# One pair's x by DMA transpose instead of TensorE, and a q transpose moved behind it in SP's queue

## Chip, cores and metric

One core of one Trainium2 chip. The metric is the device time of one execution in microseconds (us), taken over several executions, of which medians and ranges are given. In the profile's lines PE is TensorE, PEld its weight loads, DVE VectorE, ACT ScalarE, POOL GpSimd and SP SyncE, which issues most DMAs; a q behind the name means the engine's sequencer or its DMA queue. PSUM is the memory that TensorE writes its results to.

## The reference

Sliding-window attention over 8 batches and 8 heads, its output taken as 4608 rows of 512, and a two-layer network with an ELU on top. Cut to what matters:

```python
# q, k, v: (8, 8, 576, 64); |i - j| <= 32 may attend
scores = 1.0 / np.sqrt(D) * np.matmul(q, k.transpose(0, 1, 3, 2))
attn = softmax(np.where(mask, scores, -1e9))           # (written out in the reference)
x = (attn @ v).transpose(0, 2, 1, 3).reshape(B * S, H * D)      # (4608, 512)
h = x @ w_in                                           # (4608, 2048)
g = np.where(h > 0.0, h, np.exp(np.minimum(h, 0.0)) - 1.0)
out = g @ w_out                                        # (4608, 512)
```

## The kernel before

The network's work is 144 loop steps, eight for each tile of 256 rows. In each step TensorE does a first-layer block of eight matmuls (`mm1`), and a second-layer block of four (`mm2`) for the step two back. ScalarE makes the exponential `e_sb`, VectorE `m_sb` and `g_sb` of it. Attention runs ahead of the network in the gaps. It goes by pairs, a pair being 128 rows; two pairs make the x of one tile. `begin` says at which step a pair's scores are made; three or four steps later it is normalized, and its x (128 x 512) must be transposed, either on TensorE with a ScalarE copy out of PSUM, or by a DMA on SP's queue:

```python
    FIRST_TWO, FIRST_DMA, BACK_AT = 6, 10, 18
    begin = {4: 9, 5: 12, 6: 18, 8: 26, 10: 31, 12: 37}
    # ... (cut)
    for i in range(4, NPAIR):
        # ... (cut: scores, exponential, mask, pv of the pair)
        n = kk + (3 + z if two else 2)
        at(n, "dve", normalize, i)
        if i < FIRST_DMA:
            at(n, "end", x_transpose, i)         # four TensorE transposes
            at(n, "end", x_evac, i, nc.scalar)   # ScalarE copies PSUM to SBUF
        else:
            at(n, "end", x_dma, i)               # one DMA transpose on SP
```

Pair 8 begins at step 26 and is normalized at step 29, pair 9 at step 30. Their tile is first read at step 32. The q and k of a later batch are cast, written to DRAM and brought back transposed by a DMA on SP:

```python
            if j0 == 12:
                at(free[n], "end", write_rows, b, which)
                at(free[n] + (3 if free[n] == 29 else 4), "mid",
                   transpose_rows, b, which)
```

For batch 3, q is written at step 24 and k at step 29, so their transposes are issued at steps 28 and 32.

The softmax here doesn't subtract the row's maximum and nothing guards it: scores larger than these inputs give would overflow.

## Time and profile before

| | before |
|---|---|
| device time, median of 3 executions | 305.11 us (304.83 to 305.93) |
| profiled execution (a fourth one, of 306.17 us), span in the trace | 304.5 us |
| TensorE busy | 296.0 us, 97% |
| TensorE's share of the chain that ended last | 90% |

The first table row is the metric. The span is the profiled execution as the trace sees it, from the first instruction to the last; it is some 1.7 us shorter than the device time of the same execution. The chain that ended last is followed back from the last instruction, at each step to what released it. As 90% of it is TensorE's work, what is taken from other engines only counts where TensorE waits for them. The lines behind this, and those of steps 28 to 32, are in the prediction.

### The profile page before, as it was taken

Reading aid. Unit: us, or ns where it says so; the run is one execution under the profiler, and the core shown is the slowest. Engines: PE = TensorE matmul, PEld = TensorE weight load, DVE = VectorE, ACT = ScalarE, POOL = GpSimd, SP = SyncE. Lnnn points to the kernel's source line nnn. Section 1 sums busy time; section 2 is a strip of 40 time slices with the busy share of each in tenths; the row PEclk is TensorE's granted clock in tenths of the full one; section 3 lists DMA queues with packets and bytes.
Section 4 is the critical chain, followed back from the end, with each engine's and each line's share of the span. In section 5 each row is a group of like instructions: output and inputs, shape, how many; then the busy total and the mean of one; then the engine's idle time right before and its main releaser. Section 6 shows DMA issues by size and latency. Waiting matters only on the chain.

```text
span 304.5 us, 7644 instructions
## 1 busy us (share of the span) xinstructions
PE 296.0 (97%) x3091; PEld 197.4 (65%) x3091; DVE 242.2 (80%) x473; ACT 168.6 (55%) x254; POOL 48.6 (16%) x68
## 2 busy tenths in 40 slices
PE   8789999999999999999999999999999999999995
PEld 3456666677676666666666666666667666666662
DVE  6867688978888887988798879887988787877664
ACT  3654556778664567546754675467535353534331
POOL 8836100910003100230013001400000000000000
PEclk9999999999999999999999999999999999999999
DMA  9999999998755997999799969996921111111011
GB/s 191 177 201 205 183 272 413 295 168 182 177 176 158 297 126 187 246 319 157 164 251 303 196 157 268 325 159 116 281 57 71 34 71 34 72 37 69 2 69 70
DMA packets 92117, 52.81 MB, mean 173 GB/s; under 512 B 76594, under 2 KB 81970, under 8 KB 92082
## 3 DMA queue, kind: packets, MB, share of 16 engines
q1 hardware_dynamic: 47330, 35.61, 43.3%
q0 software_dynamic: 42880, 10.10, 40.9%
q10 hardware_dynamic: 1872, 6.62, 5.8%
q8 instruction: 24, 0.39, 0.6%
q14 instruction: 11, 0.09, 0.1%
HBM read 36.70 MB, written 15.34 MB: 171 GB/s over the span
## 4 chain that ended last, share of the span: by engine, by line
PE 90%; DMA 3%; DVE 2%; POOL 2%; ACT 1%; issue 1%; DVEq 0%; POOLq 0%; ACTq 0%
PE ps L602 41%; PE psY L640 40%; PE psS L336 4%; PE psS L304 3%; DMA w_in_sb<-in_moe_w_in_dram 3%; PE ptx L279 1%; POOL Ve L142 1%; POOL c L136 1%; PE psXT L357 1%; DVE g_sb L626 1%; ACT pu L315 1%; DVE pm L324 0%; DVE m_sb L615 0%; PE ptx L274 0%; ACT e_sb L609 0%
## 5 line engine op out<-in xcount | busy, mean ns | idle before, releaser
L609 ACT ACTIVATE e_sb<-ps 128x512 f32<-128x512 f32 (+1 forms) x145 | 86.3, 595 | 120.6 <-PE ps L602 113.0
L602 PE MATMUL ps<-xT,w_in_sb 128*128 128x256 bf16 x1152 | 149.2, 273 | 1.4 <-DMA w_in_sb<-in_moe_w_in_dram 1.4
L640 PE MATMUL psY<-w_out_sb,g_sb 128*128 128x512 bf16 x576 | 147.6, 380 | 0.2 <-DVE g_sb L626 0.2
L602 PEld LDWEIGHTS <-w_in_sb 128*128 128x128 bf16 x1152 | 110.6, 98 | 39.7 <-DMA w_in_sb<-in_moe_w_in_dram 1.9
L626 DVE SCALAR_TENSOR_TENSOR g_sb<-ps,m_sb 128x512 bf16<-128x512 f32 (+1 forms) x145 | 99.4, 686 | 12.6
L615 DVE TENSOR_SCALAR m_sb<-e_sb 128x512 bf16<-128x512 f32 x144 | 62.5, 434 | 38.3 <-ACT e_sb L609 36.5
L640 PEld LDWEIGHTS <-g_sb 128*128 128x128 bf16 x576 | 54.5, 98 | 39.0 <-DVE g_sb L626 0.6
L142 POOL DMA_DIRECT2D Ve<-in_v_dram x40 | 35.4, 897 | 139.7 <-PE psS L336 79.9
L315 ACT ACTIVATE pu<-psS 128x1024 bf16<-128x1024 f32 x36 | 36.5, 1021 | 1.4 <-PE psS L304 1.4
L348 DVE TENSOR_TENSOR x_st<-psS,rc 128x512 bf16<-128x512 f32 x36 | 24.9, 692 | 1.2
L324 DVE TENSOR_TENSOR pm<-pu,masks 128x1024 bf16<-128x1024 bf16 x36 | 24.6, 683 | 0.6 <-ACT pu L315 0.5
L234 ACT CAST qkb<-f 128x768 bf16<-128x768 f32 (+1 forms) x29 | 25.0, 860 | 0.0
L336 PEld LDWEIGHTS <-pm 128*64 128x64 bf16 x576 | 11.2, 111 | 9.9 <-DVE pm L324 8.7
L336 PE MATMUL psS<-Ve,pm 128*64 128x65 bf16 x320 | 13.6, 197 | 0.9 <-DVE pm L324 0.9
L236 DVE COPY y_sb<-psY 128x512 f32<-128x512 f32 (+1 forms) x19 | 12.7, 671 | 1.0 <-PE psY L640 1.0
L304 PEld LDWEIGHTS <-kT 64*128 64x128 bf16 x576 | 9.5, 95 | 4.9 <-issue 4.0
L336 PE MATMUL psS<-Vo,pm 128*64 128x65 bf16 x256 | 12.0, 196 | 0.2 <-DVE Vo L153 0.2
L304 PE MATMUL psS<-qT,kT 64*128 64x64 bf16 x576 | 11.8, 191 | 0.5 <-DVE kT L236 0.5
L234 ACT COPY y_sb<-psY 128x512 f32<-128x512 f32 (+1 forms) x18 | 10.3, 571 | 3.0 <-DVE y_sb L236 3.0
L153 DVE COPY Vo<-Ve 64x1040 bf16<-64x1040 bf16 x24 | 10.3, 431 | 1.5 <-DMA Ve<-in_v_dram 0.8
L395 PE MATMUL ps_idle<-zeros 128*128 128x512 bf16 x27 | 9.5, 482 | 1.3 <-DVE zeros L194 1.3
L234 ACT COPY qT<-ptx 128x1152 bf16<-128x1152 bf16 (+2 forms) x8 | 7.5, 971 | 3.9 <-PE ptx L279 3.0
(36 smaller groups left out, 72.4 us busy)
## 6 DMA issues: line engine op xcount, KB each, us to landing
out_dram<-y_sb SPq DMA_DIRECT2D x35, 256.0 KB, 3.5
f<-in_q_dram SPq DMA_DIRECT2D x12, 576.0 KB, 5.6
f<-in_k_dram SPq DMA_DIRECT2D x12, 576.0 KB, 7.9
in_dram<-qkb ACTq DMA_DIRECT2D x10, 576.0 KB, 3.9
Ve<-in_v_dram POOLq DMA_DIRECT2D x24, 128.0 KB, 11.0
w_in_sb<-in_moe_w_in_dram POOLq DMA_DIRECT2D x4, 512.0 KB, 9.9
w_out_sb<-in_moe_w_out_dram POOLq DMA_DIRECT2D x4, 512.0 KB, 12.8
Ve<-in_v_dram POOLq DMA_DIRECT2D x16, 96.0 KB, 10.5
```

The source lines that it names most:

```text
L142: nc.gpsimd.dma_start(out=V_e[b % 3][p0:p1, m, :, 0:D], in_=v[b, :, lo + p0:lo + p1, :].rearrange("h p d -> p h d"))
L234: nc.scalar.copy(d_, s_)
L304: nc.tensor.matmul(psS[:, h % 2, hp * 128 + z * QB:hp * 128 + (z + 1) * QB], lhsT=kT[b % 2][base:base + 64, KPAD + hp * S + QB * qb - WIN: ...
L315: nc.scalar.activation(pu, _bap(psS, [psS.ap[0], [1, 1024]]), AX.Exp, scale=SCALE)
L324: nc.vector.tensor_mul(pm, pu, _bap(mm, [mm.ap[0], [0, H], [1, 2 * QB]]))
L336: nc.tensor.matmul(psS[QB * z:QB * (z + 1), par, hp * VD:(hp + 1) * VD], lhsT=pm[:, par * HP + hp, z * QB:(z + 1) * QB], rhs=vv[:, qb // 2 ...
L348: nc.vector.tensor_mul(x_st, _bap(psS, [psS.ap[0], [VD, HP], [512, 2], [1, D]]), _bap(rc, [rc.ap[0], [2, HP], [1, 2], [0, D]]))
L602: nc.tensor.matmul(ps[:, j, :], lhsT=w_in_sb[:, do, fo * 128:(fo + 1) * 128], rhs=xT[t][:, :, do, :], start=(do == 0), stop=(do == NDO - 1))
L609: nc.scalar.activation(e_sb, ps, AX.Exp)
L615: nc.vector.tensor_scalar(m_sb, e_sb, -1.0, None, ALU.add)
L626: nc.vector.scalar_tensor_tensor(g_t[kk][:, z * w:(z + 1) * w, :], ps, 0.0, m_t[kk][z], ALU.max, ALU.min)
L640: nc.tensor.matmul(psY[t][ts], lhsT=g_t[kk][:, j, ts * 128:(ts + 1) * 128], rhs=w_out_sb[:, s * FG + j, :], start=(s == 0 and j == 0), sto ...
```

## The change

The intent is to take four transposes off TensorE, which is the bound, and a copy off ScalarE. SP's queue is idle where the new DMA goes, and batch 3's q transpose, which holds it for 3.4 us just before, is put behind it.

```diff
         n = kk + (3 + z if two else 2)
         at(n, "dve", normalize, i)
-        if i < FIRST_DMA:
+        if i < FIRST_DMA and i != 8:
             at(n, "end", x_transpose, i)
             at(n, "end", x_evac, i, nc.scalar)
         else:
@@
-                at(free[n] + (3 if free[n] == 29 else 4), "mid",
+
+                at({24: 30, 29: 32}.get(free[n], free[n] + 4), "mid",
                    transpose_rows, b, which)
```

Only batch 3's q moves, from step 28 to 30. The empty line makes the line numbers after it greater by one: L602 of before is L603 of after, and so on.

## The prediction

> **What bounds the kernel now.** First the page: which engine is full, and what the chain that ended last is made of.
>
> ```profile
> PE 296.0 (97%) x3091; PEld 197.4 (65%) x3091; DVE 242.2 (80%) x473; ACT 168.6 (55%) x254; POOL 48.6 (16%) x68
> PE 90%; DMA 3%; DVE 2%; POOL 2%; ACT 1%; issue 1%; DVEq 0%; POOLq 0%; ACTq 0%
> ```
>
> TensorE is the bound: 90% of the chain is its own work, and outside the first 40 us it hardly ever stands still. So in the middle of the kernel the only things that count are the time its instructions take and the short waits between them. The change touches one place in the middle: loop steps 28 to 32. A step is one first-layer block (8 matmuls, L602), one second-layer block (4 matmuls, L640) and, in some steps, attention work. I found the steps from the program's order: the output copies of tile 2 end step 25, those of tile 3 step 33. So the block at 79.63 us is the first-layer block of step 29, those at 81.60, 83.70 and 86.17 are of steps 30, 31 and 32, and step 32 is the first that reads x of pairs 8 and 9 (tile 4).
>
> Second, the chain in order of time over these steps (start us, us, what). It gives TensorE's blocks with their pipelining taken out, so the pieces add up.
>
> ```profile
> 79.70 0.98 PE ps L602 x8
> 80.68 0.86 PE psY L640 x4
> 81.54 0.22 PE psXT L357 x4
> 81.77 0.87 PE ps L602 x8
> 82.64 0.86 PE psY L640 x4
> 83.50 0.36 PE psXT L357 x4
> 83.86 0.87 PE ps L602 x8
> 84.73 0.63 PE psS L304 x32
> ```
>
> The piece at 81.54 is the four transposes of pair 8, 0.22 us; the change takes it away. The piece at 83.50 is the same four transposes for pair 9, yet it lasts 0.36 us. The extra 0.14 us is a wait: TensorE arrives there before the data.
>
> Third, VectorE's timeline over the same time (start us, us, engine, line), to see when pair 9's x is made:
>
> ```profile
> 80.28 0.69 DVE L348 TENSOR_TENSOR x_st<-psS,rc 128x512 bf16<-128x512 f32 x1
> 81.34 0.43 DVE L615 TENSOR_SCALAR m_sb<-e_sb 128x512 bf16<-128x512 f32 x1 [0.37 <-ACT e_sb L609]
> 81.88 0.69 DVE L626 SCALAR_TENSOR_TENSOR g_sb<-ps,m_sb 128x512 bf16<-128x512 f32 x1
> 82.48 0.20 DVE L345 RECIPROCAL rc<-psS 128x8 f32<-128x8 f32 x1
> 82.72 0.69 DVE L348 TENSOR_TENSOR x_st<-psS,rc 128x512 bf16<-128x512 f32 x1
> ```
>
> Pair 8's x ends at 80.97. Pair 9's ends at 83.41, at the end of a chain that begins with step 29's first-layer block: its exponential on ScalarE (80.72 to 81.32), m_sb, g_sb, reciprocal, x_st. The weight load of pair 9's transposes then starts at 83.46, and the waits of this window (us in total, times, longest us) give how long the weight loader had stood:
>
> ```profile
> PEld L357 <- DVE x_st L348: 0.5, 1, 0.5
> ```
>
> Fourth, the SP queue's timeline:
>
> ```profile
> 76.68 3.44 SPq L265 DMA_TRANSPOSE qT<-in_dram  x1
> 86.36 1.96 SPq L265 DMA_TRANSPOSE kT<-in_dram  x1
> 90.08 0.93 SPq L665 DMA_DIRECT2D out_dram<-y_sb  x2
> 92.10 3.27 SPq L374 DMA_TRANSPOSE xT<-x_st  x2
> ```
>
> The queue is free from 80.12 to 86.36.
>
> **What the Trainium skill says.** "VectorE: DVE Perf Modes", The three transpose paths, puts a 128x128 bf16 transpose at 390 ns on TensorE, into PSUM, and at 1309 ns by DMA, into SBUF. The trace has TensorE shorter: 218 ns each, and four overlap to 0.22 us. For a DMA transpose of a pair it has 1.19 to 1.95 us of the issuing queue and 2.4 to 9.2 us to landing, median 2.8. So the DMA costs more time but no TensorE time. "DMA: Bandwidth & Descriptors", Issuing engines are not separate DMA queues, says that DMAs of all issuers share the same 16 engines and interleave. The trace agrees: x transposes issued in a quiet stretch land in 2.4 to 3.5 us, the one issued at 103.9 us, with 576 KB loads under way, in 6.4. [...]
>
> **The change, part by part.**
>
> *Removed on TensorE:* four transposes of pair 8, 0.22 us on the chain. *Removed on ScalarE:* the copy of pair 8 out of PSUM, 0.58 us at 81.80, with some 0.1 us of idle time in front of the cast behind it gone too.
>
> *What becomes of the 0.22 us.* Step 30's first-layer block starts at 81.54 in place of 81.77 and ends at 82.41; the second-layer block ends at 83.28. Then come pair 9's transposes, which need pair 9's x at 83.41. Does that x come earlier? Its chain starts from the end of step 29's first-layer block, which lies before the removed transposes, and nothing removed lies on it: step 29's exponential starts before the removed copy, and VectorE's five instructions stay. Worked out: block end 80.68, exponential done 81.32, m_sb 81.77, g_sb 82.57, reciprocal 82.68, x_st 83.41: 2.73 us, and 0.05 to the weight load. TensorE needs 0.86 + 0.87 + 0.86 = 2.59 us between the same two points without the removed transposes, 2.81 with them. So the wait that was 0.14 becomes 0.36, and the transposes of pair 9 stand where they stood: gain so far **0.00 us**.
>
> *What ScalarE's 0.6 to 0.7 us give.* The cast (0.84) moves from 82.28 to about 81.37, the write of k's rows to DRAM (0.57 on ScalarE's queue) from 83.15 to about 82.25, step 30's exponential from 83.83 to about 82.9. In the kernel before, that exponential (to 84.43) stands in front of pair 9's copy out of PSUM, which so ends at 84.90, while the scores of pair 11, into the same PSUM buffer, are due halfway through the piece at 84.73. That piece takes 0.63 us; the same 32 matmuls take 0.57 at 74.04, 96.63 and 106.86. After the change the copy can start at about 83.9 and end at 84.5, ahead of the scores: gain **0.06 us**.
>
> *Added on SP:* one DMA transpose, about 1.2 us of the queue, from 81.0. Nothing large is in flight then: the q transpose that was has moved, the batch-3 v loads were issued by 62 us and the next input loads come at 95.4. By the quiet cases it lands 2.4 to 3.5 us later, at 83.4 to 84.5. Step 32 needs it at 86.17, so 1.7 us are in hand: **0.00 us** on the path.
>
> *Moved on SP:* batch 3's q transpose, from 76.68 to about 82.2, behind x. Its issue (3.44) ends at 85.6, before k's transpose can start at 86.36 (which waits for the rows of k, written from about 82.25 rather than 83.15, and 3.9 us to landing in the median). With the median 5.9 us q lands at 88.1, k by about 91. The scores of pairs 12 and 13, the first to read them, come at 96.63. **0.00 us**.
>
> Sum: 305.11 - 0.06 = **305.05 us**. TensorE's work falls by 0.22 us, but 0.22 us of waiting takes its place.
>
> **Rivals.** *The whole 0.22 us counts, or 0.28 with the scores:* 304.8. For it: TensorE is the bound and the transposes are on the chain. Against it: the wait for pair 9's x 2 us later, already 0.14 us long. *The DMA is late:* x lands after 86.17. For it: landings up to 9.2 us are in this trace, and one of 6.4 from 81.0 gives 87.4, 1.2 us late: 306.3; 9.2 would give about 309. Against it: those fell among large loads; DMA moved 0 GB/s from 82 to 84 us. *The q transpose or the write of k's rows, now together, hold k up:* the write competes with q's 576 KB; SP's k would then start at 88 or 89 and push the output at 90.08 by a little. There are some 5 us in hand before the scores, so 305.1 still.
>
> **Range and chances.** The three runs spread over 1.1 us (304.83 to 305.93), which is more than the effect. I take 304.5 to 305.7: the low end is the first rival with the noise, the high end the noise and a little lateness. 2% is 6.1 us. Nothing in the change could give that much (the removed work is under 1 us on any engine), and only a landing later than any seen here could cost it: faster 0.005, same 0.985, slower 0.01.
>
> **What would show each step.** In the changed profile's chain the piece of pair 9's transposes grows from 0.36 to about 0.58 (wait plus work), with the weight load's wait for x_st from 0.5 to about 0.7; if it stays at 0.36 or shrinks, the step on the wait is wrong and the rival of 0.22 us holds. The scores piece shrinks from 0.63 to 0.57. ScalarE's exponential of step 30 starts some 0.9 us earlier against step 29's block. The new x transpose is at about 81.0 on SP and lands within 3.5 us; a wait of step 32's first-layer block for a DMA would show the late-DMA rival. The prediction fails as a time below 304.5 or above 305.7.

## The result and the profile after

| | before | after |
|---|---|---|
| device time, median of 5 executions each | 305.2 us (304.83 to 305.93) | 306.35 us (305.95 to 306.82) |
| ratio after to before | | 1.0036, 95% interval 1.0018 to 1.0053 |
| span of the profiled execution | 304.5 us | 304.6 us |

A ratio is the mean time of one kernel's fast runs over that of the other's of the same rounds, so it is not quite the ratio of the medians quoted. The two count as "same" (within 2%), as predicted, but the time lies above the predicted range: the change costs where a gain of 0.06 us was predicted. The results are correct. The spans differ by so little because the profiled execution of before happened to start slowly, as is shown below.

The page's busy line and chain shares of the kernel after:

```profile
PE 292.2 (96%) x3034; PEld 197.0 (65%) x3087; DVE 242.9 (80%) x473; ACT 168.4 (55%) x253; POOL 48.2 (16%) x68
PE 87%; DVE 4%; DMA 3%; POOL 2%; issue 2%; ACT 1%; DVEq 0%; POOLq 0%
```

The weight loads (PEld) tell what was removed: 3087 for 3091, four transposes. ScalarE has one instruction fewer. Of the 57 matmuls that PE seems to have lost, four are the removed transposes and the others missing records: a second trace of the kernel before has 3038.

**At the place of the change nearly all goes as the prediction has it.** The chain of the kernel after in order of time (start us, us, what):

```profile
79.14 0.99 PE ps L603 x8
...
80.16 0.61 ACT e_sb L610
...
80.79 0.44 DVE m_sb L616
...
81.32 0.69 DVE g_sb L627
82.01 0.12 DVE rc L345
...
82.16 0.70 DVE x_st L348
...
82.91 0.40 PE psXT L357 x4
83.31 0.87 PE ps L603 x8
84.18 0.57 PE psS L304 x32
```

The removed piece is gone. The chain now leaves TensorE at the end of step 29's first-layer block and runs through ScalarE and VectorE to pair 9's x (`x_st`), because TensorE now waits for this x. For that reason the piece of pair 9's transposes shows 0.40 us and not the 0.58 that the prediction gave as its sign: the chain counts the wait as VectorE's work. The weight loader's wait in the same stretch (us in total, times, longest us), 0.5 us before, is longer:

```profile
PEld L357 <- DVE x_st L348: 0.7, 1, 0.7
```

The scores piece shrank from 0.63 to 0.57 us, as predicted. SP's queue of the kernel after (start us, us, engine, line):

```profile
80.45 1.30 SPq L374 DMA_TRANSPOSE xT<-x_st  x1
81.86 4.15 SPq L265 DMA_TRANSPOSE qT<-in_dram  x1
86.05 2.26 SPq L265 DMA_TRANSPOSE kT<-in_dram  x1
```

The x transpose is issued at 80.45 us, and step 32's first-layer block, its first reader, starts at 85.72 right behind the work in front of it: nothing waits for the DMA. (The trace holds no landing time for this one; in p2, an experiment below, it is 3.57 us.)

**Where the time went.** To compare two traces over the whole kernel I use one marker per step: the start of that step's `g_sb` on VectorE. The difference between two kernels in the start of the same marker is constant where they run alike and jumps where one of them loses time. "c1" and "c2" are a second profile of the kernels before and after, on one chip.

| `g_sb` of step | after - before, us | c2 - c1, us |
|---|---|---|
| 29 | -0.56 | +0.58 |
| 33 | -0.61 | +0.52 |
| 61 | -0.62 | +0.53 |
| 66 | -0.50 | +0.65 |
| 95 | -0.39 | +0.76 |
| the last (step 143, second half) | -0.40 | +0.75 |
| end of the span | +0.16 | +1.29 |

The first row is the two kernels' different luck in the start-up, before the changed steps; it differs in sign between the two pairs of profiles. From there on both pairs say the same: a gain of 0.05 us at the place of the change, two losses of some 0.11 us around steps 62 and 91, and a loss of about half a us after the last marker. Together after loses 0.72 us in both pairs, none of it where the change is.

**The stall on VectorE.** VectorE's timeline at step 62 (start us, us, engine, line, operation; in brackets the idle time in front, and what the profile puts it down to). Before:

```profile
146.79 0.43 DVE L615 TENSOR_SCALAR m_sb<-e_sb 128x512 bf16<-128x512 f32 x1
147.33 0.69 DVE L626 SCALAR_TENSOR_TENSOR g_sb<-ps,m_sb 128x512 bf16<-128x512 f32 x1
```

After:

```profile
146.18 0.43 DVE L616 TENSOR_SCALAR m_sb<-e_sb 128x512 bf16<-128x512 f32 x1
147.06 0.69 DVE L627 SCALAR_TENSOR_TENSOR g_sb<-ps,m_sb 128x512 bf16<-128x512 f32 x1 [0.46 <-PE ps L603]
```

From m_sb's start to g_sb's start it is 0.54 us before and 0.88 after: g_sb is 0.34 us late. The releaser in brackets is an inference of the profile, and it can't be right: the `ps` that g_sb reads was read by the exponential that m_sb comes from. The same happens at step 91 (from 0.53 to 0.89 us). As g_sb is the last to read its PSUM buffer, a first-layer block two steps on has to wait, and 0.11 us of each stall reach TensorE.

**The end.** The last transfer of both kernels is an output DMA of ScalarE's queue. Before, then after:

```profile
301.77 0.36 ACTq L657 DMA_DIRECT2D out_dram<-y_sb  x1
```

```profile
301.37 0.36 ACTq L658 DMA_DIRECT2D out_dram<-y_sb  x1
```

After is 0.40 us ahead here, and ends 0.16 us later. The semaphore checks of SP on the kernel's last line show why (engine, operation, count: duration in ns, first and last start in us). Before, in the stretch 301.6 to 302.1 and then 303.0 to 303.8:

```profile
L712 SPq EVENT_SEMAPHORE  x6: 17/28/28, 301.7 to 302.0; - x6
...
L712 SPq EVENT_SEMAPHORE  x2: 28/28/28, 303.2 to 303.6; - x2
```

After, in the stretch 303.0 to 303.8; between 301.4 and 303.1 there is none:

```profile
L713 SPq EVENT_SEMAPHORE  x8: 28/28/28, 303.2 to 303.6; - x8
```

SP checks at the end that every DMA has completed, one semaphore after another in a fixed order. Before, it gets through most of them while the last output is in flight, and the last check passes as that output lands. After, it stands at the first check until the output lands, and has all others still to do. The traces name the semaphores: SP's checks go through 100, 102, 104, 105 and 115 to 118 in this order, and the last output is on 118 in the kernel before and on 100 in the kernel after. The waits of SP's queue over the end (us in total, times, longest us), before and after:

```profile
SPq L712 <- DMA out_dram<-y_sb: 1.4, 3, 0.7
```

```profile
SPq L713 <- DMA out_dram<-y_sb: 1.8, 1, 1.8
```

One wait in place of three is the sign that I looked for in the experiments. A second thing is late at the end: ScalarE's last DRAIN (a sequencer instruction), before and after, in the same form as SP's lines above:

```profile
L712 ACTq DRAIN  x1: 8/8/8, 303.9 to 303.9; - x1
```

```profile
L713 ACTq DRAIN  x1: 135/135/135, 304.3 to 304.3; - x1
```

### The profile page after: what moved, and what is told of

It is laid out like the page before. It is cut to its first block, busy times and chain, and to the rows that moved or that the text cites. A ratio compares the mean times of both kernels' runs of the same rounds, so it can differ in the third digit from the quotient of the medians.

```text
span 304.6 us, 7584 instructions
## 1 busy us (share of the span) xinstructions
PE 292.2 (96%) x3034; PEld 197.0 (65%) x3087; DVE 242.9 (80%) x473; ACT 168.4 (55%) x253; POOL 48.2 (16%) x68
## 3 DMA queue, kind: packets, MB, share of 16 engines
q1 hardware_dynamic: 47874, 35.74, 43.5%
## 4 chain that ended last, share of the span: by engine, by line
PE 87%; DVE 4%; DMA 3%; POOL 2%; issue 2%; ACT 1%; DVEq 0%; POOLq 0%
PE ps L603 40%; PE psY L641 38%; PE psS L336 4%; PE psS L304 3%; DMA w_in_sb<-in_moe_w_in_dram 3%; DVE g_sb L627 1%; PE ptx L279 1%; POOL Ve L142 1%; ACT e_sb L610 1%; DVE m_sb L616 1%; POOL c L136 1%; PE psXT L357 1%; DVE x_st L348 0%; DVE pm L324 0%; DVE Vo L153 0%
## 5 line engine op out<-in xcount | busy, mean ns | idle before, releaser
L603 PE MATMUL ps<-xT,w_in_sb 128*128 128x256 bf16 x1152 | 149.2, 273 | 0.3 <-DMA w_in_sb<-in_moe_w_in_dram 0.2
L641 PE MATMUL psY<-w_out_sb,g_sb 128*128 128x512 bf16 x526 | 139.3, 379 | 3.3 <-issue 0.8
L603 PEld LDWEIGHTS <-w_in_sb 128*128 128x128 bf16 x1152 | 110.8, 98 | 38.8 <-DMA w_in_sb<-in_moe_w_in_dram 0.7
L616 DVE TENSOR_SCALAR m_sb<-e_sb 128x512 bf16<-128x512 f32 x144 | 63.2, 439 | 36.2 <-ACT e_sb L610 34.3
L395 PE MATMUL ps_idle<-zeros 128*128 128x512 bf16 x24 | 8.6, 470 | 1.4 <-DVE zeros L194 1.3
```

Source lines behind the costliest of these rows:

```text
L603: nc.tensor.matmul(ps[:, j, :], lhsT=w_in_sb[:, do, fo * 128:(fo + 1) * 128], rhs=xT[t][:, :, do, :], start=(do == 0), stop=(do == NDO - 1))
L616: nc.vector.tensor_scalar(m_sb, e_sb, -1.0, None, ALU.add)
L641: nc.tensor.matmul(psY[t][ts], lhsT=g_t[kk][:, j, ts * 128:(ts + 1) * 128], rhs=w_out_sb[:, s * FG + j, :], start=(s == 0 and j == 0), sto ...
```

## The experiments

**My theory** after reading the traces: both losses come from how the program is numbered, not from the work. The compiled program's listing, which isn't printed here, shows that the DMAs of SP and ScalarE signal completion on eight semaphores in turn, in program order; the change adds one DMA at step 29, so every later DMA moves on by one, which the semaphores named above bear out. That puts the last output from the semaphore that SP checks last onto the one that it checks first. And the change alters which waits VectorE's instructions need. In the traces only EVENT_SEMAPHORE instructions carry two waits (28 in before); any other carries one, and a further one costs an EVENT_SEMAPHORE in front of it. So VectorE's own instruction count shifts: by this listing the g_sb of steps 62 and 91 are its instructions 316 and 445 before, and 318 and 446 after. VectorE's records in the traces, counted from the first, give two more each (318 and 447, 320 and 448). They show where the shift comes from: after has one more EVENT_SEMAPHORE at 89.7 us, where pair 10's x waits for the DMA that reads pair 8's (semaphore 115), one more at 105.2 us, and one fewer between steps 62 and 91. p2 below has the same three, f1 none of them, so this is not the turn of the semaphores alone. 318 and 446 are 128 apart, which suggested a limit in the instruction stream. **The rivals:** it is the moved q transpose; it is the DMA of x itself (traffic, or TensorE's freed time shifting everything); or it is chance.

In the table, the tail is the time from the last marker's start to the end of the span, and the body from step 12's marker to the last one, both from the profiled execution's records. "Start" is the mean over the kernel's timed runs of what is left of the span, on the assumption that tail and body are the same in every run. The ratio is to the kernel before on the same chip. Rows between two lines of dashes ran on one chip.

| run | tail | body | start | median time | ratio, 95% interval |
|---|---|---|---|---|---|
| c1_before_again | 5.33 | 254.46 | 44.08 | 305.54 | 1.0002, 0.9983 to 1.0020 |
| c2_after_again | 5.87 | 254.64 | 43.96 | 306.22 | 1.0022, 1.0001 to 1.0042 |
| p1_q_moved_only | 5.33 | 254.48 | 43.93 | 305.36 | 0.9998, 0.9979 to 1.0017 |
| p2_x_by_dma_only | 5.88 | 254.65 | 44.47 | 306.85 | 1.0042, 1.0019 to 1.0064 |
| - | | | | | |
| f1_one_more_dma | 5.75 | 254.45 | 43.78 | 305.60 | 1.0011, 0.9999 to 1.0023 |
| f2_two_memsets | 5.32 | 254.58 | 43.84 | 305.41 | 1.0003, 0.9990 to 1.0016 |
| f5_after_memset | 5.88 | 254.41 | 44.20 | 306.27 | 1.0028, 1.0008 to 1.0049 |
| f4_after_memset_7dmas | 5.34 | 254.42 | 44.26 | 305.86 | 1.0016, 1.0002 to 1.0029 |
| - | | | | | |
| g1_same_length | 5.33 | 254.42 | 43.77 | 305.31 | 0.9996, 0.9980 to 1.0012 |
| g2_f4_again | 5.33 | 254.42 | 43.92 | 305.47 | 1.0000, 0.9983 to 1.0016 |
| h1_before_pair9_later | 5.33 | 254.51 | 43.93 | 305.38 | 1.0002, 0.9984 to 1.0019 |
| h2_f4_pair9_later | 5.33 | 254.29 | 44.01 | 305.38 | 1.0001, 0.9984 to 1.0018 |
| - | | | | | |
| i1_after_third | 5.88 | 254.65 | 43.47 | 305.63 | 1.0014, 1.0001 to 1.0027 |
| i2_after_padded | 5.75 | 254.65 | 43.95 | 306.17 | 1.0024, 1.0009 to 1.0039 |
| i3_before_padded | 5.32 | 254.49 | 43.60 | 305.17 | 0.9993, 0.9981 to 1.0005 |

Tail and body repeat to within 0.05 us from run to run of the same kernel; the start does not (43.5 to 44.5). That is why the verdicts rest on the first two columns, and the times only check their sum.

### The parts alone, and both kernels again

c1 is the kernel before unchanged and c2 the kernel after unchanged. p1 has only the second half of the diff, p2 only the first:

```diff
# p1
-                at(free[n] + (3 if free[n] == 29 else 4), "mid",
+                at({24: 30, 29: 32}.get(free[n], free[n] + 4), "mid",
# p2
-        if i < FIRST_DMA:
+        if i < FIRST_DMA and i != 8:
```

> Control: the kernel before under another name, on the chip and in the rounds of the other three runs. Theory N (the 1.15 us between the two kernels is mostly between chips, sessions or start-ups, not between programs): this run is as far from the kernel before as the others are, some 0.1 to 0.3%. Theory P (the programs really differ): ratio 1.000 within 0.1%, and the times 304.8 to 305.9 us.

> The whole change again, beside the control. Theory N: ratio below 1.002, near the control's. Theory P: ratio 1.003 to 1.005 again, some 306.3 us, with the control at 1.000. In the trace, either way: the weight load of pair 9's transposes waits 0.7 us for x, and steps 30 to 33 run 0.06 us shorter than before.

> Only the q transpose of batch 3 moved from step 28 to step 30; pair 8's x stays on TensorE. If the move of the q transpose is what costs (it then runs beside the write of k's rows and moves what follows on the queue), 306.2 us, ratio 1.003 or more. If the x by DMA costs, or the length of TensorE's and ScalarE's programs, 305.2 us, ratio 1.000. Theory N: as the control.

> Only pair 8's x by DMA, the q transpose left in front of it in the queue. If the x by DMA or the shorter programs of TensorE and ScalarE cost, 306.2 us, ratio 1.003 or more; if the move of q costs, 305.1. Theory N: as the control. The q transpose's issue ends at 80.1 us, before x is ready at 81.0, so x should be issued at 81.0 all the same, and land behind q's last packets, by about 84.

p1 is like before in all columns (tail 5.33, body 254.48): moving q costs nothing. p2 has both losses whole (5.88, 254.65), with its g_sb of step 62 late by the same amount (m_sb at 146.13, g_sb at 147.01). So the loss belongs to the first half of the diff, pair 8's x by DMA, and the rival of the moved q falls. c1 and c2 repeat the difference of tail and body, so chance does not make it. p2 also shows that q need not have moved: its x transpose is issued at 80.40 us, as soon as x is made.

### One DMA more, and nothing else

f1 is the kernel before with one DMA of 2 bytes on SP's queue at step 18. TensorE, ScalarE and x are untouched.

```diff
+    for _ in range(1):
+        at(18, "mid", gate, w_in_at(3))
```

> The kernel before with one DMA of 2 bytes more on SP's queue at step 18; TensorE's, ScalarE's and VectorE's programs as before. Theory L (the completion semaphores of SP's and ScalarE's DMAs go round eight; one DMA more turns the round by one, so that the very last output's is the first and not the last that SP checks at the end, and the other checks, 0.055 us each, come after it): the stretch from the last g_sb's start to the end of the span grows from 5.35 to 5.8 us, with no stall at steps 62 and 91; time +0.45 us, ratio 1.0015. Theory D (the shorter programs of TensorE or ScalarE cost the 0.7 us): no change, 5.35 us.

The waits of SP's queue over the end, in f1:

```profile
SPq L715 <- DMA out_dram<-y_sb: 1.8, 1, 1.8
```

The tail rises from 5.33 to 5.75 us, with the one long wait of the kernel after and the last output on semaphore 100, as there. A DMA of two bytes, some 250 us before the end, costs 0.42 us at the end. This is neither the traffic of x nor TensorE's freed time, only the turn in which semaphores are given out. The body is unchanged, and step 62 does not stall: VectorE's numbers at step 62 are those of before.

### VectorE's instruction count, and nothing else

f2 is the kernel before with two memsets of one element on VectorE at step 40, which by the listing puts step 62's g_sb at 318 and step 91's at 447. f5 is the kernel after with one such memset, for 319 and 447.

```diff
# f2: before, with
+    pad = cpool.tile([1, 1], BF16, name="pad")
+    for _ in range(2):
+        at(40, "dve", nc.vector.memset, pad, 0.0)
# f5: after, with the same and range(1)
```

> The kernel before with two memsets of one element on VectorE at step 40, nothing else. Theory F (VectorE stands still some 0.35 us at fixed counts of its own instructions, which shows only where that count falls between an instruction's semaphore wait and the instruction: count 318 and 446, by the programs' listings, in the changed kernel the g_sb of steps 62 and 91): the g_sb of step 62 is now number 318 and starts 0.35 us late, that of step 91 is 447 and doesn't; net some 0.1 us. Rival (the stalls come from the x transpose by DMA or from TensorE's shorter program): no stall at 62. The tail stays at 5.35 us. Time within noise, ratio 1.000 to 1.0005.

> The whole change with one memset of one element on VectorE at step 40. Theory F: g_sb of steps 62 and 91 are now numbers 319 and 447 and both stalls are gone; the body is then 0.06 us shorter than the kernel before from step 33 to the last g_sb. Theory L: the tail stays at 5.88 us. Time some 305.8, ratio 1.001 to 1.002. Rival: the stalls stay, as x is still transposed by DMA.

VectorE's timeline at step 62, of f2 and then of f5:

```profile
145.55 0.43 DVE L619 TENSOR_SCALAR m_sb<-e_sb 128x512 bf16<-128x512 f32 x1
146.43 0.69 DVE L630 SCALAR_TENSOR_TENSOR g_sb<-ps,m_sb 128x512 bf16<-128x512 f32 x1 [0.46 <-PE ps L606]
```

```profile
145.43 0.43 DVE L619 TENSOR_SCALAR m_sb<-e_sb 128x512 bf16<-128x512 f32 x1
145.96 0.69 DVE L630 SCALAR_TENSOR_TENSOR g_sb<-ps,m_sb 128x512 bf16<-128x512 f32 x1
```

f2 has x on TensorE and no further DMA, and stalls at step 62 all the same (0.88 us from m_sb to g_sb); at step 91, where its count is 447, it does not. f5 has the DMA and stalls nowhere: adding an instruction to the kernel after takes 0.23 us off its body (254.64 to 254.41). So the stall is a matter of the instruction's place in VectorE's program. Its size in the body is 0.12 us for one (f2 against c1 over step 62) and 0.23 for two. f5's time, 306.27 us, is 0.5 us over what was expected; the excess is in its start (44.20).

What lies behind it is less certain. The Trainium skill ("Runtime: NRT & Kernel Launch", Instruction fetch mechanics) has engines fetch their program through a DMA queue of their own, in 16 KiB blocks of 256 instructions, and calls the cost of crossing a block mostly hidden. By these figures of the page an instruction would be 64 bytes, an estimate. The trace has such fetches: a DMA queue of kind "instruction" moves single packets of about 8 KB (10 in the kernel after, 0.08 MB), which at 64 bytes is 128 instructions, just the distance of the two stalls. The line of it in the DMA view of the kernel after, from 144 to 150 us (packets, MB, share of the 16 engines):

```profile
q14 instruction: 1, 0.01, 0.3%
```

Narrowing the stretch places this packet relative to step 62's g_sb: 1.68 to 1.71 us after it in before, c1, p1 and f1 (count 316), 1.29 to 1.33 us after it in after, c2, f2 and i2 (318), and 0.69 us ahead of it in f5 and f4 (319). One VectorE instruction more moves the packet by two us, so it belongs to VectorE's program, and to this place in it. By listing and traces, in all the stalled cases the boundary falls between g_sb and the EVENT_SEMAPHORE instruction that holds one of its two waits, where no other wait can hide it. But the packet lands after the stall, so it is not what g_sb waited for; around step 91 its place is less regular.

The traces hold a third case. The late DRAIN at the end is record 448 of ScalarE, the number that the stalled g_sb of step 91 has among VectorE's records in the kernel after. It is so in all five kernels where it is late (after, c2, p2, f5, i1; it takes 121 to 136 ns). In the twelve other traces it is record 449 or 450 and takes 8 to 14 ns. So the late DRAIN too goes with an instruction's number on its engine. Not every 64th record stalls, though 320 and 448 are multiples of 64: f5's VectorE record 256 and f2's 640 are each a g_sb with its EVENT_SEMAPHORE in front, and start 45 ns after it as usual.

That the number matters is thus shown; that an engine passing from one block of its program to the next stands for 0.35 us, and that this is the fetch of its program, is argued.

### Both mended

f4 is f5 with seven more of the 2-byte DMAs, so that with pair 8's there are eight more than before and every later DMA has its old semaphore again. It ran again as g2. g1 is f4 with four idle matmuls and a one-element ScalarE copy at the very end, to give TensorE and ScalarE back the operations that the change took out.

```diff
# f4 and g2: f5 with
+    for _ in range(7):
+        at(18, "mid", gate, w_in_at(3))
# g1: f4 with, after the last second-layer matmuls,
+                idle(4, "h1")
+                nc.scalar.copy(pad2, zeros[0:1, 0:1])
```

> The whole change with the memset and with seven DMAs of 2 bytes on SP's queue at step 18, so that the round of eight semaphores ends as in the kernel before. Theories F and L together: no stalls, a tail of 5.35 us, and the 0.06 us gained in steps 30 to 33 is left: some 305.3, ratio 0.9995 to 1.0005. If the 1 us stays, neither theory holds.

> What is left open: with its stalls and its tail mended (f4) the changed kernel's body and tail are as short as before, and its runs were still some 0.4 us longer, which must lie in the start, before the change. This is that kernel with four idle matmuls and one ScalarE copy at the very end, so that TensorE's and ScalarE's programs are as long as before. If the length of the programs is what makes the start longer (their place in memory moves), 305.3 us, ratio 1.000; if not, 305.8 as f4.

> f4 again (the change, a memset, seven DMAs), beside g1, to see whether its 305.86 us holds. If the start really is longer: 305.7 to 305.9, ratio 1.001 to 1.002. If it was chance: 305.3.

The waits of SP's queue over the end, in f4:

```profile
SPq L718 <- DMA out_dram<-y_sb: 1.4, 3, 0.7
```

Seven DMAs more, and the tail is back at 5.34 us, with the three waits of the kernel before. Together f1 and f4 settle the end: one more DMA breaks it, eight more leave it whole. Body and tail of f4, g1 and g2 sum to some 0.03 us less than c1's and 0.05 less than before's, against the 0.06 that the prediction has for the whole change. The times of g1 and g2 are those of before (0.9996, 1.0000). In its first series f4 stood at 1.0016, 0.5 us over its expected time, with its start at 44.26; g2, the same kernel, has 43.92. So that excess was not in body or tail, and it did not repeat.

### Is the saved 0.22 us really lost to the wait for pair 9?

The prediction says that the time freed on TensorE turns into a longer wait for pair 9's x. If so, giving pair 9's transposes a later place in TensorE's program, behind work that is ready, must set it free. h2 does that on f4: the transposes go behind step 31's first-layer block, and pair 11's scores to the end of that step. h1 is the same edit on the kernel before.

```diff
-        at(kk, "end" if i == 4 else "mid", scores, i,
+        at(kk, "end" if i in (4, 11) else "mid", scores, i,
@@
-            at(n, "end", x_transpose, i)
-            at(n, "end", x_evac, i, nc.scalar)
+            m = (n + 1, "mid") if i == 9 else (n, "end")
+            at(*m, x_transpose, i)
+            at(*m, x_evac, i, nc.scalar)
```

> The kernel before with pair 9's transposes put behind step 31's first-layer block, and pair 11's scores at the end of step 31, so that TensorE doesn't wait for pair 9's x (0.14 us) nor for its copy (0.06 us); one more change from scores to matmuls costs some 0.1 us (the block after scores lasts 0.97 in place of 0.86). So 0.1 us less than before in the trace, 305.3, ratio 0.9995; no stalls at 62 and 91, tail 5.35.

> f4 with pair 9's transposes and pair 11's scores put later in the same way: if the 0.22 us saved on TensorE was lost to the wait for pair 9's x, and to nothing else, it is won here: 0.3 us less than the kernel before between the g_sb of step 29 and that of step 33, and until the end of the span; time 305.0 if the start is as before, 305.5 if it is f4's.

The chain of h2 in order of time (start us, us, what):

```profile
82.74 0.87 PE ps L609 x8
83.61 0.22 PE psXT L357 x4
83.84 0.34 PE psS L304 x16
84.18 0.97 PE psY L647 x4
85.15 0.34 PE psS L304 x16
```

Pair 9's transposes now take 0.22 us, their bare time, and the chain stays on TensorE. Against c1, h2's marker goes from +0.10 us at step 29 to -0.10 at step 33: 0.20 us gained, where 0.3 was expected. h1's goes from +0.67 to +0.69: nothing gained, where 0.1 was expected. The edit is the same, so the 0.22 us between them are the four transposes that h2 does not have. The scores in two pieces take 0.68 us, not 0.57, which is why h1 gains nothing from its shorter wait. So the step of the prediction on the wait is shown. h2 has the shortest body of all (254.29), yet its time is that of before (1.0001): 0.2 us is 0.06% and below what six executions resolve. No kernel here is measurably faster than the kernel before.

### Why the first series showed more than the traces

Body and tail account for about 0.7 us, and the first series had 1.15 between the medians. I asked whether the rest is real, say from a program of another length. i1 is the kernel after a third time; i2 and i3 are after and before with g1's padding at the end.

```diff
# i1: the kernel after, unchanged
# i2: after, i3: before, each with
+                idle(4, "h1")
+                nc.scalar.copy(pad2, zeros[0:1, 0:1])
```

> The changed kernel a third time, beside the two padded ones. Its body and tail are fixed (0.18 and 0.53 us over the kernel before in the traces); what is looked for is the start, the time until the g_sb of step 12, worked out for each timed run as its span less body and tail: 44.1 to 44.2 us if the start is longer in this program, against some 43.9 in the kernel before.

> The changed kernel with four idle matmuls and one ScalarE copy at the very end, so that the programs of TensorE and ScalarE are as long as before; stalls at 62 and 91 and the long tail stay. If program length makes the start longer: start 43.9 us, time 305.9. If it doesn't, or if the start differs only by chance: as i1.

> The kernel before with the same five instructions more at the end, so its programs are longer than before by what the changed ones are shorter. If the start depends on program length or place: a start other than 43.9 by over 0.2 us. If only chance: 43.8 to 44.0 us, time 305.3, ratio 1.000.

i1 has the tail and body of its earlier runs, but a start of 43.47 us, and is at 1.0014. The mean differences of the unchanged kernel after to before in its three series are 1.08, 0.68 and 0.42 us, 0.73 in the mean: what the traces sum to. Over all its runs the start is 43.83 us (17 runs, standard error 0.11), and 43.87 (33 runs, 0.06) in the kernels with x on TensorE. So the excess of the first series fits chance in the start. It isn't shown to be that. The starts of p2 (44.47), f4 (44.26) and f5 (44.20) are high too, and all three have pair 8's x by DMA. All 58 runs of such kernels give 44.01 us (0.07), and all 77 runs with x on TensorE, the kernel before beside the last four series included, 43.88 (0.04): 0.13 us apart, with a standard error of 0.08. An effect of that size in the start stays open. Nor does padding settle it: i3's start, 43.60, falls below the 43.8 to 44.0 that was set down for chance, but i1's without padding is lower still, and i2's is 43.95. Padding shortens the tail of after from 5.88 to 5.75 us, f1's value, because ScalarE's last DRAIN is then record 449 and no longer late.

## Why the prediction was wrong

*Held.* The chain around pair 9's transposes, the weight loader's wait (0.7 us predicted and measured), the scores at 0.57 us, the exponential of step 30 earlier against step 29's block (by 1.1 us, 0.9 predicted), x in place before its first reader, the q transpose at 0.00 (p1: 0.9998). Locally after is 0.05 to 0.06 us ahead of before at step 33, for 0.06 predicted. The rival that all 0.22 us count is refuted by c2 and by h2 against h1; that of the late DMA by step 32 running without a wait. One sum doesn't add up as written: 2.78 us to the weight load less 2.59 leaves a wait of 0.19, not 0.36. The two sums end at different points. The piece of 0.36 runs to the end of pair 9's transposes, which comes 0.45 us after x is made in both traces (83.41 to 83.86, and 82.86 to 83.31); what matters, that the wait grows by the 0.22 us taken out in front of it, is right.

*Failed.* The step "**Added on SP:** one DMA transpose ... **0.00 us** on the path". It asked only when this DMA is issued and lands. It did not ask what one DMA more in program order does to all those behind it, nor what reading x by a DMA does to the waits, and so the instruction counts, of the other engines. The sum has no term outside steps 28 to 33. In place of 0.00 the runs show:

| term | predicted | measured | shown by |
|---|---|---|---|
| steps 28 to 33 | -0.06 | -0.05 to -0.06 | both pairs of traces |
| VectorE's count at steps 62 and 91 | none | +0.22 to +0.23 | f2, f5 |
| order of the last checks on SP | none | +0.42 | f1, f4 |
| ScalarE's late last DRAIN | none | +0.13 | i2, f4; late only as record 448 |
| sum | -0.06 | +0.72 in the traces, +0.73 in time | |

Before plus this sum is 305.9 us, above the upper end of 305.7. The other 0.4 us of the 306.35 lie in that series' starts, by chance as far as is known. That too is a fault of the range: the three runs it was drawn from spread over 1.1 us, and the upper end left only 0.65 us for noise and error together.

The expected gain thus has a clear fate. Of 0.22 us of TensorE's work, all went into the wait for pair 9's x; 0.06 us came from ScalarE's freed time (read from the traces, no run isolates it); and three losses far from pair 8's steps cost more than ten times that.

## What to carry to other kernels

In a program like this one, a DMA added or removed shifts the completion semaphores of all DMAs behind it, and with them which transfer the last checks end on. Giving a buffer to another engine or a DMA changes waits, and so instruction counts. Look at the end of the trace and compare one marker per step over the whole kernel, not only at the place of the change. Work saved in front of a wait was lost to that wait here until something that was ready took its place. Effects under 0.3% are found in the traces' constant parts; the times of a handful of executions, whose start alone has a standard deviation of some 0.4 us, can only confirm the sum.

## What the Trainium skill lacked or had wrong

- "Runtime: NRT & Kernel Launch", Instruction fetch mechanics, and "Advanced Engine Details and Errata", ISA Cache: blocks of 16 KiB or 256 instructions; the first calls crossing one mostly hidden. One queue of fetches agrees with the size (24 packets, 0.39 MB, so 16 KB each; at 64 bytes 6144 instructions, near the 6222 records of TensorE, so it is taken to be TensorE's). The packet that follows VectorE's count is about 8 KB, the two stalls lie 128 instructions apart, and each delays its instruction by 0.35 us, of which 0.11 us reach the end. ScalarE's record 448 is late as well and costs 0.13 us. If these counts are block boundaries, crossing them is not always hidden; the link between fetch and stall is argued.
- None of the pages says that the DMAs of SP and ScalarE in a program like this share eight completion semaphores in turn, or that SP checks them in a fixed order at the end: the same last output costs 0.42 us more at the end if it is on the one checked first (tail 5.33 and 5.75 us in c1 and f1).
- "VectorE: DVE Perf Modes", The three transpose paths, compares the duration of one transpose. Here four on TensorE cost 0.22 us on the chain, and taking them away gave nothing until the next wait had other work in front of it (h2 against h1: 0.22 us).
